# Sixty constant products in TensorE's early waits, and the turn of the outputs made on 64x128 tiles, once per group

## The chip, the core and the metric

The kernel runs on one core of a Trainium2 chip. Its engines are TensorE (PE, with the weight loads shown as PEld), VectorE (DVE), ScalarE (ACT), GpSimd (POOL) and SyncE (SP, which here only issues DMAs). Each engine works through its own queue in order, and steps on different engines are tied by semaphores. The metric is the device time of one execution in microseconds; smaller is better.

## What is computed

A gated linear attention runs over 768 tokens for 4 batches of 8 heads of width 48, and its output is the input of a feed-forward layer whose hidden value is the largest of three products.

```python
for t in range(S):
    state = alpha[:, :, t, :, None] * state + einsum('bhd,bhe->bhde', k[:, :, t], v[:, :, t])
    y[:, :, t] = einsum('bhd,bhde->bhe', q[:, :, t], state)
x = y.transpose(0, 2, 1, 3).reshape(B * S, H * D)        # 3072 x 384
h = maximum(maximum(x @ w1, x @ w2), x @ w3)             # 3072 x 768
out = h @ w_out                                          # 3072 x 384
```

## The kernel before

The work is cut into 12 groups of 256 tokens (three chunks of time by four batches, `n = 4 * c + b`). A group is two blocks of 128 tokens. The attention is done in chunks of 64 steps: decays become sums of logarithms, and q and k are scaled by their exponentials, so that a chunk is a masked product.

Each group goes through these kinds of steps. The short names are those of the code.

- `load` (SP, line 274): a, q, k, v of a group, 384 KB each; group 0 in halves of four heads.
- `aa`, `la` (351, 356, 361): the product of neighbouring decays, and logarithms. `hp` (371), `e` (378), `G` (383, 388): the totals of a chunk and their exponentials.
- `Lp` (426, a product with a constant triangle), `L0` (430), `exp` (435, ep and en), `qk` (440, on GpSimd or VectorE), `v` (259 or 261): one of two units of four heads.
- `tp` (465): turns q and k; from group 2 on both units in one step. `qkT` (479) copies that out of PSUM. `A` (491) are the scores and `LA` (499) masks them.
- `pp` (523): what the group adds to the state; `Z` (400) and `add` (412) carry the state on.
- `yi` (556) and `ya` (578): the output from the state and from the scores. `xb` (259 or 261) copies and scales a block of it; `xp` (599) turns that block with a constant matrix `order`, in three products; `xT` (255) copies the turned block.
- `gp` (622): products with the weights. The kernel uses max(x w1, x w2, x w3) = x w1 + max(0, x (w2 - w1), x (w3 - w1)): `d` (308) are the two differences, `h0` (631 or 633) and `h1` (638) the maximum, and x w1 w_out is added by `past`, a product of w1 and w_out worked out once (`wt` 322, `w1T`, `mp` 334).
- `op` (655 and 658): the last product, `ob` (255) its copy, `out` (674) the store.

`weights` (288, 291) are the four weight loads, issued on GpSimd and cast on the way: w1s (weights 0), the two halves of wcat (1 and 2), wo (3).

The order of the work isn't found by the program: the string `ORDER` lists every step with its engine and its PSUM bank (`28P0` is step 28 on TensorE, bank 0), and `Plan.emit` issues them so. There are eight banks, and a step that writes a bank waits until its last reader is done. Within an engine the order in the string is the order of its queue. Before the first `gp` TensorE has the attention of groups 0 and 1 up to the turned outputs, the first steps of group 2 and two of the three `wt`.

Of the kernel before, what the change touches and what calls it, by code (L numbers as in the profile page):

```python
# [10 lines left out]
FP32 = mybir.dt.float32  # L11
FP16 = mybir.dt.float16

AOP = mybir.AluOpType
# [9 lines left out]


ORDER = """
0S 3S 53S 6S 7S 5S 2S 1S 11V 12A 8V 13A 4S 10A 28P0 9A 54S 14P1 29V 17P2 57V 55S 30A 18V 31A 56S
59A 33V 100S 58A 60P3 75P4 19A 102S 63P5 76V 34A 101S 32V 61A 20A 103S 64V 35P6 15A 22V 145S 21V
207S 23A 36V 24P2 148S 65A 16V 40P01 146S 25V 77A 78A 147S 67G 26P6 41V 66A 275S 37P2 39G 79V 343S
42V 209S 38V 80G 208S 277S 74G 82P4 68V 69A 278S 70P2 62G 86G 210S 83V 45P0 276S 71V 81G 27V 104G  # L30
72P4 87P23 73V 46P6 50A 89V 84P4 47A 88V 85V 106A 92P7 48P0 105A 411S 49V 93P2 51P6 94V 97A 110P4
90V 98P5 111V 117P0 107P7 44V 197P2 108A 91V 52A 195P7 189V 112A 95P3 99A 118V 257P6 113A 190V 120A
261P5 258V 96A 196A 191V 325P4 122V 262A 265P3 43V 115G 119A 199P6 266A 329P7 131G 326A 121V 200A
114V 194V 124P0 116A 193V 333P5 125V 123A 330A 128V 126P3 149G 334A 132P67 127V 129P0 150A 331P5
109G 151A 198A 134V 335P3 133V 130V 162P4 137P6 267P2 163V 152P0 263P1 332V 165A 153A 192V 164A
138P5 154G 336V 259P0 211G 139A 136V 155P4 205P3 156V 213A 168G 142V 157A 203P5 161A 135V 260V 158A
166G 220P6 212A 327P7 264V 204A 143P4 268V 159G 214P0 140P1 144A 201P5 221V 141A 167V 215A 206A
227P2 393P4 160V 202A 217G 228V 169P0 279G 328V 229A 176P35 230A 173V 269P7 219G 223A 178V 347G
281A 170V 394A 177V 222A 282P2 174P0 180V 283A 225G 171P3 270A 337P6 175V 280A 232G 611S 172V 345S
288P2 181P7 224G 338A 295P0 272P1 348A 296V 231G 289V 297A 179V 349A 182P6 285V 298A 287V 234P3  # L40
291A 216V 273V 286G 340P5 183A 218G 238V 186A 274S 300G 290A 235V 344S 363P0 239P6 677S 341A 233G
364V 397P1 294A 240V 346S 226G 187P2 479S 350P3 299G 398A 399P4 545S 351A 236P5 188A 293G 400V 414S
241P71 301A 184P3 342S 401P2 242V 185A 284G 243V 413S 237V 366A 403P4 245G 402A 412S 244G 356P7
465P3 292G 480S 247V 309P25 357V 481S 466A 467P6 404V 415G 365A 548S 246V 249P3 359A 248P4 339S
310V 302P0 358A 368G 468V 546S 417A 250P 311V 416A 482S 469P7 353G 306V 313G 251A 271S 312G 461P6
303V 254A 614S 360G 470A 315V 418P2 307P3 547S 314V 462A 304P0 252P7 308V 367G 419A 255P5 463P6
253A 256A 361G 316P2 305V 317P7 362A 395P3 369G 471P4 464V 421G 352G 431P5 318P 355G 472V 354G
370P0 322A 423G 535P6 374V 319A 483G 424P4 527P7 396V 536A 549G 531P2 371V 528A 377P36 425V 430G
551A 375P0 408P7 378V 532A 379V 380G 432V 485A 381G 376V 434A 426A 533P3 436G 433A 382V 492P2 427A
372P0 383V 422G 552P5 484A 320P4 476P6 429G 493V 534V 495A 428G 321A 373V 494A 537P3 477A 435G  # L50
323P4 616A 529P2 409V 324A 538V 385P6 553A 558P0 384P1 550A 486P7 438P4 530V 487A 386P 489G 488V
437G 559V 499P3 565P7 387A 473P2 420V 390V 497G 561A 500V 439V 615G 501A 388P1 405P6 474A 566V 389A
442V 502A 491V 560A 391P2 504G 440P4 392A 593P1 441V 555G 490G 597P3 594A 445P02 568A 443P4 598A
659P1 447V 446V 617A 449G 444V 599P3 406A 496G 407S 663P0 681V 475S 661P6 664A 563V 678S 539P4 660A
498G 600V 410S 683A 564G 612S 567A 448V 618P5 679S 562G 665P0 450V 540V 680S 667P1 451V 505G 541S
666V 631P3 452P7 668A 595P4 613S 632V 619A 503V 624P2 634A 453P0 684P1 513P5 596V 621G 633A 570G
454P 685A 682A 515V 506P3 662V 458A 571G 669P1 455A 625V 635G 514V 627A 459P0 601P6 507V 626A 569G
460A 456P7 670V 542P5 602A 510V 554G 557G 628G 511P0 543A 508P2 579P6 512V 457A 630G 544S 572P4
556G 725P7 516V 509V 687G 729P0 629G 726A 603P1 730A 689G 580V 518P7 731P2 517V 581V 636G 690P3
573V 674P0 691V 582G 576V 637G 519P6 732V 583G 638P4 675A 693A 604V 520P 676S 697P0 622V 727P2 521A  # L60
524V 692A 733P1 698V 639V 699A 522P7 605P6 523A 728V 701G 734A 642V 688G 577P2 606A 574P4 585P7
578V 700A 607S 525P1 671P6 702G 526A 478S 575V 623G 584P0 703G 735P1 672A 696A 694G 673S 586P 736V
645P2 620G 643P3 686G 640P5 646V 608P1 647V 587V 641V 751P2 609A 644V 590A 740P0 610S 591P5 743P6
592V 588P1 649V 747P7 589A 648V 752V 741A 650P3 651P4 765P5 742S 695V 652P 744V 704P0 653A 711P2
656A 769P6 712V 766A 713V 657P3 705V 654P4 715G 770A 737P2 708V 658A 748A 714V 655A 706P5 709P0
717P3 707V 779P7 749P4 780A 710V 787P5 716P6 750V 763P7 718P 753P0 745P1 754V 789P4 719V 761P0 746V
783P6 722V 762A 767P1 764V 723P3 755P0 724V 738V 784V 720P7 758P3 721V 797P2 759V 771P6 788V 760S
805P7 756V 772V 785P3 757S 798V 739S 801P5 806V 781P0 768V 803P6 802V 773P2 790V 804V 799P7 782V
807P1 786V 776P5 800V 808V 791P4 774V 777V 775S 778S 813P6 792V 809P0 793S 817P3 814P 810P 815V
818P 794P7 811A 816S 812S 819V 820S 795A 796S  # L70
"""


# [41 lines left out]
def kernel(  # L115
# [12 lines left out]
    nc = tc.nc  # L128
# [14 lines left out]
    NG = NU // UB  # L143
    HG = UB * H
    TG = UB * P
    assert DM == H * D and NT == B * S


# [22 lines left out]
    ident, order, maskA = d16[:, :P], d16[:, P:2 * P], d16[:, 2 * P:]  # L171
# [9 lines left out]
    NL, NQ, NT_, HH = 5, 6, 4, H // 2  # L181
# [9 lines left out]
    xbs = homes(3, [P, P, NFT], FP16, "xb")  # L191
# [15 lines left out]
    nc.vector.memset(d16[:, :2 * P], 0.0)  # L207
    nc.vector.memset(maskA, 1.0)

    def keep(where, pattern, base, test, fill, step=-1):  # L210
# [9 lines left out]
    keep(order, [[1, P]], 0, AOP.not_equal, 1.0, -2)  # L220
    keep(order, [[1, P]], P - 1, AOP.not_equal, 1.0, -2)
    for t in las:
        nc.vector.memset(t[:, :, :, D:], 0.0)
    for t in qks:
# [55 lines left out]
    def weights(g):  # L280


        w, dst = ((moe_w1, moe_w2, moe_w3, moe_w_out)[g],
                  (w1s, wcat[:, 0], wcat[:, 1], wo16)[g])

        def run(eng):
            if g == 3:
                nc.gpsimd.dma_start(dst.rearrange("p (b s) f -> p b (s f)", s=2),
                                    w.rearrange("(b p s) f -> p b (s f)", p=P, s=2))
            else:  # L290
                nc.gpsimd.dma_start(dst.rearrange("p t f -> p (t f)"),
                                    w.rearrange("(p t) f -> p (t f)", t=NFT))
# [250 lines left out]
    def output(n):  # L543
# [42 lines left out]
                  + [("v16", u % NQ) for u in us])  # L586
        for i in range(UB):
            m = 2 * n + i
            xb, yk, xk = xbs[m % 3], keys[i], ("xp", n, i)
            plan.step("xb", "ACT DVE", rank,  # L590
                      lambda eng, xb=xb, yk=yk: scaled(
                          eng, xb.rearrange("p f t -> p (f t)"),
                          live[yk].rearrange("p a b -> p (a b)"), ysc),
                      reads=[yk], writes=[("xb", m % 3)])

            def turn(eng, xb=xb, xk=xk):
                live[xk] = bank(xk, [P, NFT, P], FP32)
                for ft in range(NFT):
                    nc.tensor.matmul(live[xk][:, ft, :], xb[:, :, ft], order,  # L599
                                     start=True, stop=True)  # L600

            plan.step("xp", "PE", rank, turn, banks=[xk], reads=[("xb", m % 3)], writes=[xk])
            to = xTs[n][:, :, i * P:(i + 1) * P]
            plan.step("xT", "DVE ACT", rank, lambda eng, to=to, xk=xk: copy(eng, to, live[xk]),
                      reads=[xk], writes=[("xT", n, i)])


    def ffn(n):
# [31 lines left out]
        for i in range(UB):  # L640
# [5 lines left out]
            for half in range(wide):  # L646
# [3 lines left out]
                for lo, hi in parts:  # L650
                    def shrink(eng, i=i, ok=ok, lo=lo, hi=hi, cols=cols):
# [5 lines left out]
                        for kt in range(lo, hi):  # L657
# [17 lines left out]
                              out[rows, cols], obs[home][:, cols]),  # L675
                          reads=[("ob", home)], size=1 / wide)

    load(0, 0, HH, "aqk")
    load(0, HH, H, "a")
    load(0, 0, HH, "v")  # L680
# [50 lines left out]
```

## Time and profile before

| | us |
|---|---|
| median of three runs | 150.99 |
| the three runs | 150.17, 150.99, 152.28 |
| span of the profiled execution | 148.5 |

The profiled execution has its span alone, from the first to the last instruction; its own device time is not listed, and the three runs lie 1.7 to 3.8 us above that span.

In the profile a row of a group reads: line, engine, operation, what it writes and reads, shapes and count; then the time busy in us, the mean of one in ns, and the idle time of the engine just before, with what ended it. In a timeline a row is the start in us, how long, the engine, the line and the count, and in brackets the idle time before it. In the chain of waits a row is a start, a length and what the end hung on there.

### The profile page before, as it was taken

What the parts mean: (1) busy time and instruction counts of PE and PEld (TensorE: products, weight loads), DVE (VectorE), ACT (ScalarE), POOL (GpSimd) and SP (SyncE); (2) the same over time, 40 slices, a digit from 0 to 9 for tenths busy, and PEclk for the clock granted to TensorE, in tenths of its full rate; (3) what the DMA queues carried; (4) which work ended last, traced back from release to release, by engine and by line L of the source; (5) the groups of instructions that cost most, each with busy time, mean ns of one, the idle gap of its engine ahead of it and who ended that gap; (6) DMA issues with size and microseconds to landing.
All of it is one profiled execution on the core that took longest, in us unless ns stands there. A gap on an engine that the chain in (4) does not pass through costs nothing.

```text
span 148.5 us, 5617 instructions
## 1 busy us (share of the span) xinstructions
PE 130.6 (88%) x2389; PEld 101.7 (68%) x2389; DVE 121.9 (82%) x231; ACT 80.7 (54%) x182; POOL 71.8 (48%) x114
## 2 busy tenths in 40 slices
PE   0136588889999999999999999999999999999990
PEld 0025576767776678887687889777777788787670
DVE  6489996999899979998896899699698786789720
ACT  3665156796895987947877759328622820000011
POOL 8105810431859888999976678994720100000000
PEclk9999999999999999999999999999999999999999
DMA  4999999999999999999997299601211100031223
GB/s 111 257 261 262 258 214 212 279 231 265 270 262 265 261 275 267 262 288 268 233 279 188 79 246 280 200 3 60 106 57 57 53 4 0 4 119 40 85 99 134
DMA packets 54728, 26.34 MB, mean 177 GB/s; under 512 B 50736, under 2 KB 54320, under 8 KB 54704
## 3 DMA queue, kind: packets, MB, share of 16 engines
q1 hardware_dynamic: 53584, 23.60, 63.4%
q0 software_dynamic: 832, 2.36, 8.1%
q8 instruction: 18, 0.29, 0.9%
q10 hardware_dynamic: 288, 0.04, 0.3%
q14 instruction: 6, 0.05, 0.1%
HBM read 23.63 MB, written 4.72 MB: 191 GB/s over the span
## 4 chain that ended last, share of the span: by engine, by line
PE 65%; DMA 10%; POOL 6%; ACT 5%; DVE 4%; SPq 4%; issue 3%; POOLq 0%; DVEq 0%
PE psum L622 26%; PE psum L658 15%; PE psum L655 8%; DMA wcat<-in_moe_w_dram 6%; SPq L274 4%; DMA qn<-in_q_dram 4%; POOL qk L440 3%; PE psum L491 3%; PE psum L578 3%; PE psum L465 2%; PE psum L599 2%; PE psum L334 2%; PE psum L556 2%; PE psum L523 2%; POOL Z L400 1%
## 5 line engine op out<-in xcount | busy, mean ns | idle before, releaser
L622 PE MATMUL psum<-xT,d 128*128 128x256 f16 x432 | 54.1, 273 | 0.9 <-DVE d L308 0.5
L622 PEld LDWEIGHTS <-d 128*128 128x128 f16 x432 | 40.0, 98 | 7.0 <-DVE d L308 1.5
L499 DVE TENSOR_TENSOR LA<-psum,d 128x1024 f16<-128x1024 f32 x24 | 28.7, 1218 | 3.7 <-PE psum L491 2.8
L658 PE MATMUL psum<-wo,hT 128*128 128x384 f16 (+1 forms) x150 | 27.5, 320 | 0.0
L638 DVE TENSOR_TENSOR hT<-psum,hT 128x512 f16<-128x512 f32 x36 | 23.7, 681 | 2.9 <-PE psum L622 2.6
L440 POOL TENSOR_TENSOR qk<-qn,ep 128x384 f16<-128x384 f32 x18 | 18.3, 1026 | 11.3 <-DMA qn<-in_q_dram 9.2
L631 ACT ACTIVATE hT<-psum 128x512 f16<-128x512 f32 x28 | 16.4, 601 | 12.7 <-PE psum L622 12.3
L255 ACT COPY ob<-psum 128x384 f32<-128x384 f32 x14 | 6.7, 481 | 27.8 <-PE psum L658 27.8
L658 PEld LDWEIGHTS <-hT 128*128 128x128 f16 x150 | 14.5, 98 | 8.9
L440 POOL TENSOR_TENSOR qk<-kn,en 128x384 f16<-128x384 f32 x16 | 15.9, 999 | 9.0 <-ACT en L435 8.5
L479 DVE COPY qkT<-psum 128x1024 f16<-128x1024 f16 x24 | 16.0, 683 | 0.9 <-PE psum L465 0.7
L655 PE MATMUL psum<-past,xT 128*128 128x384 f16 (+1 forms) x75 | 15.8, 320 | 0.0
L259 ACT ACTIVATE xb<-psum,c 128x384 f16<-128x384 f32 x17 | 9.3, 583 | 9.0 <-PE psum L578 9.0
L435 ACT ACTIVATE en<-psum 128x384 f32<-128x384 f32 x24 | 11.5, 493 | 2.1 <-DVE psum L430 2.1
L465 PE MATMUL psum<-d,qk 64*128 64x64 f16 x384 | 8.8, 198 | 4.1 <-POOL qk L440 2.1
L435 ACT ACTIVATE ep<-psum 128x384 f32<-128x384 f32 x24 | 11.6, 493 | 1.1 <-DVE psum L430 0.8
L351 POOL TENSOR_TENSOR aa<-an 128x384 f32<-128x384 f32 x9 | 9.0, 1001 | 4.7 <-DVE qkT L479 4.2
L255 ACT CAST xT<-psum 128x384 f16<-128x384 f32 x20 | 9.4, 482 | 3.0 <-PE psum L599 2.8
L426 PE MATMUL psum<-la,c 128*128 128x192 f16 x24 | 6.1, 271 | 5.5 <-ACT la L361 5.5
L465 PEld LDWEIGHTS <-qk 64*128 64x128 f16 x384 | 7.0, 99 | 5.5 <-DVE qk L440 2.9
L400 POOL TENSOR_TENSOR Z<-U,G 48x192 f16<-48x192 f32 x10 | 5.0, 504 | 11.8 <-DVE U L412 11.5
L430 DVE TENSOR_TENSOR psum<-psum,la 128x192 f32<-128x192 f32 x24 | 8.5, 358 | 2.6 <-PE psum L426 1.8
(58 smaller groups left out, 196.4 us busy)
## 6 DMA issues: line engine op xcount, KB each, us to landing
out_dram<-ob SPq DMA_DIRECT2D x23, 192.0 KB, 2.0
an<-in_alpha_dram SPq DMA_DIRECT2D x11, 384.0 KB, 6.2
qn<-in_q_dram SPq DMA_DIRECT2D x11, 384.0 KB, 5.7
kn<-in_k_dram SPq DMA_DIRECT2D x11, 384.0 KB, 6.2
vn<-in_v_dram SPq DMA_DIRECT2D x11, 384.0 KB, 6.3
wcat<-in_moe_w_dram POOLq DMA_DIRECT2D x2, 576.0 KB, 10.3
w1s<-in_moe_w_dram POOLq DMA_DIRECT2D x1, 576.0 KB, 7.9
wo<-in_moe_w_out_dram POOLq DMA_DIRECT2D x1, 576.0 KB, 7.8
```

Source lines behind the costliest of these rows:

```text
L255: (nc.scalar.copy if eng == "ACT" else nc.vector.tensor_copy)(out=out, in_=in_)
L259: nc.scalar.activation(out=out, in_=in_, func=AFT.Copy, scale=factor)
L435: lambda eng, t=t, sign=sign: nc.scalar.activation(out=t, in_=live[Lk], func=AFT.Exp, scale=sign),
L440: lambda eng, w=w, x=x, e=e: on[eng].tensor_mul(qk[:, w, :, :, :D].rearrange("p r h d -> p h r d"), ld[x][n % NL][:, hs], e),
L465: nc.tensor.transpose(live["tp", v][:, i, at:at + HALF], qks[v % NQ][rows, w, r, 2 * j:2 * j + 2, :], ident[rows, rows])
L479: lambda eng: nc.vector.tensor_copy(out=qkT.rearrange("p i w j t -> p i (w j t)"), in_=live["tp", u]),
L499: lambda eng: nc.vector.tensor_mul(LA.rearrange("p a j r t -> p (a j) (r t)"), live[Ak].rearrange("p a (j t) -> p (a j) t", j=2), maskA.un ...
L622: nc.tensor.matmul(live[gk][:, jj, :], hidden(apart[g][j][:, kt], jj), xT[:, kt, :], start=(kt == 0), stop=(kt == NFT - 1))
L631: nc.scalar.activation(out=h, in_=live[gk], func=AFT.Relu)
L638: lambda eng, h=h, gk=gk: nc.vector.tensor_max(h, live[gk], h),
L655: nc.tensor.matmul(live[ok], xT[:, kt, i * P:(i + 1) * P], past[:, kt, cols], start=(kt == 0), stop=False)
L658: nc.tensor.matmul(live[ok], hT[:, kt, i * P:(i + 1) * P], wo16[:, kt, cols], start=False, stop=(kt == NJ - 1))
```

## The change

Three things change.

1. A constant tile `filler` of ones is made, and 60 steps `dm` multiply it by itself on TensorE, 128x128 by 128x256, each into a PSUM bank that nothing reads from. All 60 are placed ahead of the first `gp`.
2. The turn of the outputs is one step `xq` per group instead of two `xp`. It works with the identity on 64 rows at a time, in 12 products, into two banks; even and odd tokens come apart in the two banks, and one `xT` copy of 128x768 puts them together. The constant `order` goes, and `xb` has four buffers for three.
3. `ORDER` is a new string: engine, bank and place are new for all steps.

```diff
-    d16 = sb.tile([P, 4 * P], FP16, name="d16")
+    d16 = sb.tile([P, 3 * P], FP16, name="d16")
+    filler = sb.tile([P, TG], FP16, name="filler")
...
+    nc.vector.memset(filler, 1.0)
...
+    def fill(i):
+        key = ("dm", i)
+        plan.step("dm", "PE", -1.0,
+                  lambda eng: nc.tensor.matmul(bank(key, [P, TG], FP32), filler[:, :P], filler,
+                                               start=True, stop=True),
+                  banks=[key], writes=[key])
...
-            def turn(eng, xb=xb, xk=xk):
-                live[xk] = bank(xk, [P, NFT, P], FP32)
-                for ft in range(NFT):
-                    nc.tensor.matmul(live[xk][:, ft, :], xb[:, :, ft], order,
-                                     start=True, stop=True)
-
-            plan.step("xp", "PE", rank, turn, banks=[xk], reads=[("xb", m % 3)], writes=[xk])
-            to = xTs[n][:, :, i * P:(i + 1) * P]
-            plan.step("xT", "DVE ACT", rank, lambda eng, to=to, xk=xk: copy(eng, to, live[xk]),
-                      reads=[xk], writes=[("xT", n, i)])
+        def turn(eng):
+            live[xk] = banks2(xk, FP32)
+            for ft in range(NFT):
+                for i in range(UB):
+                    for r in range(2):
+                        rows = slice(r * HALF, (r + 1) * HALF)
+                        at = (ft * UB + i) * HALF
+                        nc.tensor.matmul(live[xk][:, r, at:at + HALF], mine[i][rows, :, ft],
+                                         ident[rows, rows], start=True, stop=True)
+
+        plan.step("xq", "PE", rank, turn, banks=[xk],
+                  reads=[("xb", (2 * n + i) % NXB) for i in range(UB)], writes=[xk])
+        to = xTs[n].rearrange("p f (i s r) -> p r (f i) s", i=UB, r=2)
+        plan.step("xT", "DVE ACT", rank,
+                  lambda eng: copy(eng, to, live[xk][:, :, :NFT * P].rearrange(
+                      "p r (a s) -> p r a s", s=HALF)),
+                  reads=[xk], writes=[("xT", n, 0), ("xT", n, 1)], size=2.0)
```

The heads of the new orders of three queues, by kind, with the group in brackets (a half, unit or pass behind the stroke):

```
SP, new:     a(0) in two halves, a(1), a(2), q(1), q(0/0), k(0/0), k(1), q(0/1), k(0/1), v(1), v(0/1), v(0/0), q(2), k(2), a(3), v(2)
SP, old:     a(0) in two halves, a(1), k(0/1), v(0/1), q(0/1), k(0/0), q(0/0), v(0/0), q(1), k(1), v(1), a(2), k(2), q(2), v(2), a(3)
GpSimd, new: G(1), weights 0, five qk of groups 1 and 0, v(1), weights 1, weights 2, v(0), weights 3, qk(2), ...
GpSimd, old: qk(1), weights 0, qk(1), weights 1, G(1), weights 2, v(1), aa(2), qk(2), weights 3, ...
TensorE, new, up to the first gp: 7 dm, hp and Lp of groups 0 and 1, 53 dm between the steps of groups 0 and 1, three wt, xq of groups 1 and 0, tp of group 2
```

More of the change, by code (lines that the diff above doesn't have):

```diff
@@ L32 @@
[L32 to L43, printed above, removed]
@@ L71 @@
+805P0 806A 754P3 797P6 798A 724V 752V 694V 753V 755P7 695P1 696A 795V 756P 757V 799P5 800V 823P2
+824A 819P3 801P1 758A 759P5 760A 817P4 807P7 808V 815P6 833P5 825P7 816A 803P6 841P2 842A 818V 820V
+837P0 821P3 802V 843P2 839P4 835P1 822V 826V 827P7 828A 834V 830P3 796S 831A 836V 804V 809P7 775S
+829S 810A 811S 832S 812P5 813A 814S 838V 840V 845P3 844V 846P 847A 848S 853P6 854P 855A 856S 849P4
+850P 851A 852S
 """
@@ L145 @@
     TG = UB * P
+    NFILL = 60
     assert DM == H * D and NT == B * S
@@ L593, in output @@
                           live[yk].rearrange("p a b -> p (a b)"), ysc),
-                      reads=[yk], writes=[("xb", m % 3)])
-            def turn(eng, xb=xb, xk=xk):
-                live[xk] = bank(xk, [P, NFT, P], FP32)
-                for ft in range(NFT):
-                    nc.tensor.matmul(live[xk][:, ft, :], xb[:, :, ft], order,
-                                     start=True, stop=True)
-            plan.step("xp", "PE", rank, turn, banks=[xk], reads=[("xb", m % 3)], writes=[xk])
-            to = xTs[n][:, :, i * P:(i + 1) * P]
-            plan.step("xT", "DVE ACT", rank, lambda eng, to=to, xk=xk: copy(eng, to, live[xk]),
-                      reads=[xk], writes=[("xT", n, i)])
+                      reads=[yk], writes=[("xb", m % NXB)])
+        xk, mine = ("xp", n), [xbs[(2 * n + i) % NXB] for i in range(UB)]
+        def turn(eng):
[14 more added lines that the diff above has]
+                  reads=[xk], writes=[("xT", n, 0), ("xT", n, 1)], size=2.0)
     def ffn(n):
@@ L676, in ffn @@
                           reads=[("ob", home)], size=1 / wide)
+    for i in range(NFILL):
+        fill(i)
     load(0, 0, HH, "aqk")
```

85 lines of the change are left out of this document (46 added, 39 removed).

## The prediction

> **What bounds the kernel now.** I read the page's busy table first, then its slices in time, then the busy time in three stretches, then the steps around the place where the stretches change.
>
> ```profile
> span 148.5 us, 5617 instructions
> PE 130.6 (88%) x2389; PEld 101.7 (68%) x2389; DVE 121.9 (82%) x231; ACT 80.7 (54%) x182; POOL 71.8 (48%) x114
> PE   0136588889999999999999999999999999999990
> PEclk9999999999999999999999999999999999999999
> DMA  4999999999999999999997299601211100031223
> ...
> 26.00:30.00 4.00, 3.52 (x34) 1.00 1.18 275
> 30.00:40.00 10.00, 9.15 (x190) 1.00 1.10 255
> 40.00:146.00 106.00, 104.90 (x1863) 1.00 0.61 157
> sum 26.00, PE 13.00; mean PE 2.60
> ...
> 26.04 0.83 PE L622 MATMUL psum<-xT,d 128*128 128x256 f16 x6 [0.51 <-DVE d L308]
> 144.20 0.99 PE psum L658 x6
> ```
>
> The kernel has two parts. Up to 26.04 us, when the first expert product (line 622) starts, TensorE is half idle: 13.00 us busy of 26. From there to the last product, which ends at 145.2 (144.20 + 0.99), it works almost without a gap: 3.52 + 9.15 + 104.90 = 117.6 us busy of 119.2, 1.6 idle. After it come 3.3 us of copy, store and end. So the span is a start (26.0), TensorE's work (117.6), its gaps (1.6) and a tail (3.3), together 148.5. A change can move the first three. The shown runs are 1.7 to 3.8 us above the span, their median 2.5; I add 2.5.
>
> What makes the start 26 us long?
>
> ```profile
> 10.00:15.00 5.00, 2.75 (x94) 2.14 (x88) 4.73 (x10) 2.14 (x5) 2.23 (x3) 1.00 1.27 263
> 15.00:20.00 5.00, 3.21 (x113) 2.78 (x117) 4.90 (x6) 0.95 (x2) 3.68 (x6) 1.00 1.19 244
> ...
> 12.73 1.38 POOL L440 TENSOR_TENSOR qk<-qn,ep 128x384 f16<-128x384 f32 x1 [8.45 <-DMA qn<-in_q_dram]
> 14.05 0.74 POOL L291 DMA_DIRECT2D w1s<-in_moe_w_dram  x1
> 15.62 0.61 ACT L259 ACTIVATE v<-vn,c 128x384 f16<-128x384 f32 x1 [2.37 <-DMA vn<-in_v_dram]
> 15.77 9.15 DMA wcat<-in_moe_w_dram
> 25.42 0.56 DVE L308 TENSOR_TENSOR d<-wcat,w1s 128x768 f16<-128x768 f16 x1 [1.18 <-DMA wcat<-in_moe_w_dram]
> q0 software_dynamic: 832, 2.36, 8.1%
> w1s<-in_moe_w_dram POOLq DMA_DIRECT2D x1, 576.0 KB, 7.9
> 17.78 11.01 SPq L274 DMA_DIRECT2D an<-in_alpha_dram  x2
> ```
>
> Columns after the stretch are the five engines PE, PEld, DVE, ACT, POOL. Two things run level: VectorE, busy 4.73 and 4.90 of each 5 us, and the DMA engines. Loads land at a steady pace: group 1's q, the end of the sixth full load in SP's order, by 12.6, and its v, the end of the eighth, by 15.6, so 1.5 us for a load. The four weight transfers take 8.1% of the engines' span, 12.0 us, 3.0 each, and they push the loads aside: SP needs 11 us from 17.78 for two issues. The last wait before the first product is VectorE's 1.18 us for wcat. TensorE is not on this chain.
>
> **The sixty products.** Seven stand ahead of all TensorE work and 53 more between there and the first expert product; none stands after it. They have 128x256 operands, as line 622 has.
>
> ```profile
> 40.36 0.65 PE psum L622 x6
> L321 PE MATMUL psum<-d,w1s x18: 219/314/314, 23.8 to 29.6; 128*128 128x128 f16 x18
> ```
>
> At 0.65/6 = 0.11 us each they are 6.5 us. The row of line 321 shows that early products are slower: 314 ns in the median and first, 219 at the fastest, while the page's granted clock reads 9 in every slice; the slices do not tell this apart. So a fill can cost up to twice 0.11, 13 us in all, about the 13.0 us that TensorE idles before 26.04. I cost them at nothing, since the idle time hides them. Without that cover they cost at most those 13 us less the idle part; the rival below prices it. [...]
>
> Each fill writes a bank of PSUM and so waits for that bank's last reader. One stands ahead of group 2's hp and two w1 turns, waiting for a masking on VectorE (line 499); hp and what is behind it use the same banks and would wait anyway. I add nothing.
>
> **The new start.** Prices from the groups by shape:
>
> ```profile
> L430 DVE TENSOR_TENSOR psum<-psum,la 128x192 f32<-128x192 f32 x24 | 8.5, 358 | 2.6 <-PE psum L426 1.8 <-ACT la L356 0.7
> L479 DVE COPY qkT<-psum 128x1024 f16<-128x1024 f16 x24 | 16.0, 683 | 0.9 <-PE psum L465 0.7
> L499 DVE TENSOR_TENSOR LA<-psum,d 128x1024 f16<-128x1024 f32 x24 | 28.7, 1218 | 3.7 <-PE psum L491 2.8 <-issue 0.7
> L440 DVE TENSOR_TENSOR qk<-kn,en 128x384 f16<-128x384 f32 x8 | 5.2, 659 | 0.0
> L440 DVE TENSOR_TENSOR qk<-qn,ep 128x384 f16<-128x384 f32 x6 | 3.2, 553 | 0.4 <-DMA qn<-in_q_dram 0.2
> L400 DVE TENSOR_TENSOR Z<-psum,G 48x192 f16<-48x192 f32 x8 | 2.8, 355 | 0.3
> L412 DVE TENSOR_TENSOR V<-psum,Z 48x192 f32<-48x192 f32 x16 | 5.5, 351 | 0.3
> L261 DVE TENSOR_SCALAR xb<-psum,c 128x384 f16<-128x384 f32 x7 | 4.3, 611 | 0.2
> L255 DVE CAST xT<-psum 128x384 f16<-128x384 f32 x4 | 2.2, 555 | 0.8 <-PE psum L599 0.8
> L255 ACT COPY w1T<-psum 128x768 f16<-128x768 f16 x3 | 2.4, 815 | 0.0
> ```
>
> VectorE first. In the new order its steps between group 0's first k half and the first d are 3 L0, 4 qkT, 4 LA, 4 qk (three q, one k), 1 w1T, 4 Z, 3 add, 2 xb. That is 3 x 0.358 + 4 x 0.683 + 4 x 1.218 + 3 x 0.553 + 0.659 + 0.6 + 4 x 0.355 + 3 x 0.351 + 2 x 0.611 = 15.3 us. (A w1T copy on VectorE is not in the trace: between 0.555, half the size from 32-bit, and 0.815 on ScalarE; I take 0.6, near the first.) That k half now ends the fifth full load's worth: two halves of alpha and one full make two, alpha of group 2 three, q of group 1 four, two halves five. So it lands one load before 12.6, at 11.1; its qk takes 0.66, and the sum ends at 27.1. In the same stretch VectorE idled 0.37 us in 10, so some 0.5 more, less about as much for the overlap of neighbours: first d at 27.1, with 26.5 and 28.5 as ends.
>
> Now the weights. GpSimd issues w1s (weights 0) right after G of group 1, before its first qk, so at about 9 us instead of 14.05. The other two are moved behind five qk and a v step on GpSimd's queue; the last of these waits for group 1's v, the eighth load as before: 15.6 plus the 3.0 us that weights 0 takes out of the loads, 18.6. With 0.6 for v the issue comes at 19.2 instead of 15.77. A weight transfer lands 7.9 us after its issue: 27.1, and VectorE starts d some 0.45 after such a landing (24.92 to 25.42), 27.5. So both lines meet; the first product follows d by 0.6 (25.42 to 26.04): **28.1 us, 2.1 later than now** (ends +0.9 and +3.5). SP's order moves alpha of group 2 and q of group 1 ahead of halves of group 0; group 1's v ends the same volume, so nothing else follows there. xT of group 0 is no later: xb ends near 25.7 in VectorE's list, then 0.2 for the turn and at most 2 x 0.48 for the copy.
>
> **TensorE's work after the first product.** Counted in the two orders from there on: 20 old turns become 10 new ones of 12 small products, one w1 turn of six products and one merged tp step of 32 go ahead of it; all else is equal.
>
> ```profile
> 43.17 0.57 PE psum L465 x32
> 45.76 0.75 PE psum L491 x32
> 48.41 0.49 PE psum L655 x3
> 50.38 0.47 PE psum L465 x32
> 50.85 0.59 PE psum L655 x3
> 53.61 0.17 PE psum L599 x3
> L255 ACT CAST xT<-psum 128x384 f16<-128x384 f32 x20 | 9.4, 482 | 3.0 <-PE psum L599 2.8
> ```
>
> An old turn is 0.17, so 20 are 3.4 us. A new product has the shape of line 465's, 64 rows by 128, 64 moving: 0.47/32 = 15 ns, 10 x 12 are 1.8 (at most 23 ns, the slowest small ones of line 491, 2.8). Gain 1.6. The w1 turn is worth 0.34 (two of 0.17), the tp 0.47.
>
> Against it stands a row: three products of line 655 take 0.49 after full-size work and 0.59 after line 465, and line 465 itself 0.47 after small work and 0.57 after line 622. So each change between full and small tile shapes costs 0.10. The old turn was full-size as its neighbours; the new one is not. Changes of shape in TensorE's order after the first product: 55 before, 64 after, 9 x 0.10 = +0.9. [...] Sum: -1.6 - 0.34 - 0.47 + 0.9 = **-1.5 us** (ends -2.4, without the changes of shape, and -0.5).
>
> The copies of xT fall from 24 to 12, all on ScalarE, each between 0.815 and 0.96 in place of two of 0.48; with VectorE's list shorter by three ob, two xb, four xT and a relu, and longer by one aa, w1T and past, VectorE loses over 4 us of work. That is off TensorE's path; it helps the 1.6 us of gaps. I take them at 0.6, **-1.0** (ends -1.6 and +0.5).
>
> **Sum:** 148.5 + 2.1 - 1.5 - 1.0 = 148.1; with 2.5 around it, 150.6: no change that can be measured. About 2% (3 us) is what a measurement can tell: three runs of the same kernel lie 1.4% apart.
>
> **Rivals.**
> *The start is not later, and the gaps close (faster).* If VectorE's list overlaps more than I allow and the w1 transfer comes with less than 7.9 us because no other weight is ahead of it, the first product stays at 26.0; the gaps go to nothing and the shape changes cost half: 148.5 - 1.9 - 1.6 = 145.0, as a run 147.5. For it: the wait at 25.42 was short, and VectorE has less to do. Against it: the later issue. Chance 0.22.
> *Group 2's k is starved (slower).* The k load stands three full loads behind group 1's v in SP's order: 18.6 + 4.5 = 23.1. The three weight transfers follow each other from about 19.2 on and take 9 us. If the first of them begins over an us before 23.1 minus its own start-up, k lands only after all three, near 31. VectorE's qk for it stands ahead of the first d, and tp of group 2 ahead of the first product, so that would start near 32.5: +6.5 - 1.5 - 1.0 = 152.5, as a run 155.0. For it: SP's 11 us for two issues. Against: weights 0 issued at 14.05 landed at 22, so 3 us of transfer started near 19, five us after the issue; the same lag puts this one at 24. Chance 0.10.
> *The fills stand in the way.* If TensorE stays slow, 13 us of fills beside 13 of work fill the start, and each step of the early chain waits behind a few: up to 2 us more: 150.1, as a run 152.6. Chance 0.13.
> *The turns gain nothing.* With products at 23 ns the work falls by 0.5 only: 149.1, as a run 151.6. Chance 0.10.
>
> **How the numbers follow.** The forecast has 0.45; it and the two last rivals lie within 2%, the first rival just past it on the fast side, half the cost of each end of the start (0.9 to 3.5) inside. Faster 0.22, same 0.67, slower 0.11. The range leaves out the starved case and the outer part of the fast one: 147.2 to 153.0.
>
> **What would show it.** In the new profile the first product of the expert group should start at 27 to 29, after a wait of VectorE for wcat of under an us or none; w1s should land well before; the fills should lie in TensorE's idle time; a turn of twelve should take 0.2 to 0.3; TensorE should be idle for under an us after the first product. A first product at 26 or before, or beyond 30, makes the sum wrong; so does TensorE work after it that is not 1 to 2 us less.

## The result and the profile after

| | before | after |
|---|---|---|
| median, us | 150.58 (150.07 to 152.28, 4 runs) | 158.97 (158.34 to 160.55, 4 runs) |
| ratio to before | 1 | 1.0538, 95% interval 1.045 to 1.0627 |
| span of the profiled execution, us | 148.5 | 157.4 (that execution as a run: 159.07) |

The change makes the kernel 5% slower; 150.6 was forecast, with 153.0 as the upper end. The page of the kernel after, its first lines and the slices of TensorE and its clock:

```profile
span 157.4 us, 5883 instructions
PE 140.3 (89%) x2521; PEld 105.0 (67%) x2521; DVE 124.0 (79%) x225; ACT 88.1 (56%) x182; POOL 69.7 (44%) x107
PE   4099896799978899998899999799999999999992
PEclk9999999869999999999999999999999999999999
```

TensorE's row has digits of 7 and 8 well into the second quarter and again in the middle, where the row of before had nines, and the clock shows an 8 and a 6 in the two slices from 27.5 to 35.4 us. Busy time by stretch of the kernel after (first column the stretch, then its length, PE, PEld, DVE, ACT, POOL, granted clock, DMA share, GB/s):

```profile
26.00:30.60 4.60, 2.04 (x63) 1.45 (x63) 2.60 (x7) 1.98 (x3) 0.00 (x0) 1.00 1.09 205
30.60:34.00 3.40, 3.04 (x16) 1.95 (x15) 3.37 (x8) 1.68 (x3) 0.66 (x1) 0.50 1.15 277
...
31.74:154.40 122.66, 118.30 (x2105) 90.41 (x2104) 101.15 (x172) 72.37 (x149) 56.25 (x81) 0.99 0.60 152
...
40.00:55.00 15.00, 12.86 (x268) 9.13 (x267) 14.71 (x27) 11.80 (x29) 8.94 (x12) 1.00 0.94 220
...
95.00:100.00 5.00, 3.87 (x58) 2.71 (x56) 4.49 (x6) 2.25 (x6) 4.85 (x10) 1.00 0.85 220
```

The first expert product (now line 642) starts at 31.74 in place of 26.04: 5.7 of the 8.9 us. From it to the end of TensorE's work the stretch is 122.66 in place of 119.16. TensorE is busy for 118.30 of it, 0.7 more than before, and idle for 4.36 in place of 1.6. The tail is 3.0 for 3.3. Together: 5.7 + 0.7 + 2.8 - 0.3 = 8.9.

The stretch from 40 to 55 shows who is late there: VectorE is busy for 14.71 of 15 us while TensorE loses 2.1. In the start, TensorE idles for over half of the 4.6 us before 30.6, then works 3.4 us at half the clock. The timeline there (start, length, engine, line, count; in brackets the idle time before):

```profile
25.43 0.55 PE L589 MATMUL psum<-v,LA 64*128 64x48 f16 x30
28.37 0.20 PE L589 MATMUL psum<-v,LA 64*128 64x48 f16 x2 [2.38 <-issue]
...
29.10 0.79 ACT L258 COPY w1T<-psum 128x768 f16<-128x768 f16 x1
...
29.78 1.91 ACT L258 CAST xT<-psum 128x768 f16<-128x768 f32 x2
...
30.37 1.03 DVE L319 TENSOR_TENSOR d<-wcat,w1s 128x768 f16<-128x768 f16 x2
...
31.74 4.52 PE L642 MATMUL psum<-xT,d 128*128 128x256 f16 x30 [0.36 <-ACT xT L258]
```

In the middle of one step (ya of group 0, 32 products) TensorE stands still for 2.38 us, and the trace names no releaser ("issue"). All that follows is late by it: xb, the turn, then on ScalarE a w1T copy and two xT copies in a row, and the first product waits for the last of these. VectorE's groups that changed most (line, operation, shapes, count; then busy us and mean ns):

```profile
L394 DVE TENSOR_TENSOR G<-e 128x4 f32<-128x4 f32 x5 | 3.7, 739 | 0.0
L399 DVE TENSOR_TENSOR H<-e,e 128x4 f32<-128x4 f32 x2 | 2.3, 1130 | 0.0
L411 DVE TENSOR_TENSOR Z<-V,H 48x192 f16<-48x192 f32 x2 | 1.9, 940 | 0.0
```

G and H have four columns and took 272 and 146 ns before; a Z from V took 350. They now take up to 1.67 us (G), 1.28 (H) and 1.22 (Z).

### The profile page after: what moved, and what is told of

Its sections match the earlier page's. It is cut to its first block, busy times and chain, and to the rows that moved or that the text cites. A ratio compares the mean times of both kernels' runs of the same rounds, so it can differ in the third digit from the quotient of the medians.

```text
span 157.4 us, 5883 instructions
## 1 busy us (share of the span) xinstructions
PE 140.3 (89%) x2521; PEld 105.0 (67%) x2521; DVE 124.0 (79%) x225; ACT 88.1 (56%) x182; POOL 69.7 (44%) x107
## 4 chain that ended last, share of the span: by engine, by line
PE 63%; DVE 17%; ACT 6%; issue 6%; DMA 3%; SPq 2%; DVEq 0%; ACTq 0%
PE psum L642 25%; PE psum L678 11%; PE psum L675 6%; DVE LA L510 4%; PE psum L303 3%; DMA qn<-in_q_dram 3%; PE psum L476 3%; PE psum L502 3%; PE psum L589 3%; SPq L277 2%; DVE hT L658 2%; ACT xT L258 2%; DVE qk L451 2%; PE psum L534 2%; PE psum L567 2%
## 5 line engine op out<-in xcount | busy, mean ns | idle before, releaser
L642 PEld LDWEIGHTS <-d 128*128 128x128 f16 x432 | 41.5, 99 | 9.4 <-issue 2.8
L651 ACT ACTIVATE hT<-psum 128x512 f16<-128x512 f32 x29 | 17.0, 600 | 21.1 <-PE psum L642 16.6
L451 POOL TENSOR_TENSOR qk<-kn,en 128x384 f16<-128x384 f32 x20 | 20.1, 1015 | 17.4 <-ACT en L446 9.3
L678 PE MATMUL psum<-wo,hT 128*128 128x384 f16 (+1 forms) x150 | 27.5, 320 | 0.0
L451 POOL TENSOR_TENSOR qk<-qn,ep 128x384 f16<-128x384 f32 x15 | 14.9, 999 | 6.5 <-ACT ep L446 3.6
L303 PE MATMUL psum<-filler 128*128 128x256 f16 x60 | 13.7, 354 | 2.1 <-DVE filler L211 1.3
L262 ACT ACTIVATE xb<-psum,c 128x384 f16<-128x384 f32 x19 | 10.3, 581 | 8.8 <-PE psum L589 8.8
L258 ACT CAST xT<-psum 128x768 f16<-128x768 f32 x12 | 12.2, 1027 | 5.0 <-PE psum L616 4.4
L258 ACT COPY ob<-psum 128x384 f32<-128x384 f32 (+1 forms) x17 | 7.7, 462 | 12.7 <-PE psum L678 11.8
L362 POOL TENSOR_TENSOR aa<-an 128x384 f32<-128x384 f32 x8 | 9.7, 1213 | 8.8 <-DMA an<-in_alpha_dram 8.8
L502 PE MATMUL psum<-qkT 48*64 48x128 f16 x384 | 8.9, 223 | 0.7 <-DVE qkT L490 0.6
```

The lines of the kernel that those rows point to most:

```text
L258: (nc.scalar.copy if eng == "ACT" else nc.vector.tensor_copy)(out=out, in_=in_)
L303: lambda eng: nc.tensor.matmul(bank(key, [P, TG], FP32), filler[:, :P], filler, start=True, stop=True),
L451: lambda eng, w=w, x=x, e=e: on[eng].tensor_mul(qk[:, w, :, :, :D].rearrange("p r h d -> p h r d"), ld[x][n % NL][:, hs], e),
L642: nc.tensor.matmul(live[gk][:, jj, :], hidden(apart[g][j][:, kt], jj), xT[:, kt, :], start=(kt == 0), stop=(kt == NFT - 1))
L651: nc.scalar.activation(out=h, in_=live[gk], func=AFT.Relu)
L678: nc.tensor.matmul(live[ok], hT[:, kt, i * P:(i + 1) * P], wo16[:, kt, cols], start=False, stop=(kt == NJ - 1))
```

## The experiments

The runs are told by cause: first the small VectorE steps, then the constant products; the turn and its copies come in between, in e9, e10 and e7. Ratios are to the kernel before, on the same chip. Spans, windows and timelines are those of one profiled execution of each run. In the diffs of `ORDER` only the entries that change are shown; they stand apart in the string.

### Small VectorE steps beside GpSimd

**e4.** Eight steps that the new order gives to VectorE (six G or H, two Z) go to GpSimd, in the same places of the order.

```diff
-269V 208V 401V 466V 469V 596V 726V 724V
+269G 208G 401G 466G 469G 596G 726G 724G
```

> The changed kernel with six small products of factors (G) and two state steps (Z) moved from VectorE back to GpSimd at the same places of the order. Theory C (contention): these steps took 0.7 to 1.4 us on VectorE where they met a GpSimd step, against 0.15 to 0.35 alone, and VectorE is what TensorE waits for at 41 to 54, 70 to 76 and 95 to 100 us; the span falls by 2 to 3 us, to 154.5 to 155.5. Rival: VectorE is late for other reasons, span 156.5 to 158.

153.18 us, ratio 1.0139 (0.9954 to 1.0324), span 152.0. Windows of this run:

```profile
31.45:149.00 117.55, 117.17 (x2105) 90.08 (x2104) 94.18 (x164) 71.85 (x149) 58.73 (x89) 0.99 0.63 159
```

Six steps at 0.15 and two at 0.35 are 1.6 us of work, but VectorE's busy time falls by 7.0, from 101.15 to 94.18, and TensorE's idle time from 4.36 to 0.4. The stop in the start stays (2.3 us). So these eight steps cost 5.4 us of span (5.8 by the medians, with two executions of e4), twice what was expected.

**e8.** The other way round in the old order: seven of the G and H steps that GpSimd has there go to VectorE.

```diff
-109G 217G 353G 352G 555G 554G 620G
+109V 217V 353V 352V 555V 554V 620V
```

> The kernel before with its own order, but seven of the fourteen small totals of a chunk (128x4, two inputs in SBUF) that GpSimd makes after the first expert product moved to VectorE, in the same places of the order. If such a step on VectorE waits until the running GpSimd step has ended, their mean goes from 0.15 us to 0.5-1.0, and the span grows by 1 to 4 us, ratio 1.01 to 1.03. If the small steps cost only their own work, 7 x 0.15 = 1 us is added on VectorE, which is idle for 18 of the 119 us, and the span grows by less than 0.5, ratio under 1.005.

150.54 us, ratio 0.9981 (0.9941 to 1.0022): the expected cost is not there. The rows of this run say why:

```profile
L383 DVE TENSOR_TENSOR G<-e 128x4 f32<-128x4 f32 x8 | 2.2, 272 | 0.0
L388 DVE TENSOR_TENSOR H<-e,e 128x4 f32<-128x4 f32 x4 | 0.6, 154 | 0.0
```

In the old order GpSimd is idle, or inside a step of at most 0.7 us, when they run; the one that met a qk (107.64) met its last 0.2 us. The engine alone is not the cause; what GpSimd does at that moment is. In the kernel after they look like this, VectorE's row and GpSimd's row in pairs:

```profile
47.81 0.98 DVE L399 TENSOR_TENSOR H<-e,e 128x4 f32<-128x4 f32 x1
47.77 1.00 POOL L451 TENSOR_TENSOR qk<-qn,ep 128x384 f16<-128x384 f32 x1 [1.56 <-ACT ep L446]
...
51.05 1.37 DVE L394 TENSOR_TENSOR G<-e 128x4 f32<-128x4 f32 x1
51.40 0.99 POOL L362 TENSOR_TENSOR aa<-an 128x384 f32<-128x384 f32 x1
```

H begins 0.04 after GpSimd's qk and ends at 48.79, 0.02 after that ends (48.77). G begins inside another qk and ends at 52.42, 0.03 after the aa that follows it (52.39): it waited through two GpSimd steps.

**e14.** Is it the reading of two tensors from SBUF that makes the step wait? In the kernel after, each G or H on VectorE becomes four products of one column, with the second factor as a scalar per partition: one tensor read from SBUF, not two.

```diff
-on[eng].tensor_mul(G, x, y)
+for j in range(NP):
+    nc.vector.tensor_scalar(out=G[:, j:j + 1], in0=x[:, j:j + 1], scalar1=y[:, j:j + 1],
+                            scalar2=1.0, op0=AOP.mult, op1=AOP.mult)
```

> The changed kernel with one thing changed: where a small total of a chunk (128x4) is made on VectorE, it is made by four products of one column each, with the second factor as a scalar per partition, so that each instruction reads one tensor from SBUF and a scalar, not two tensors. If these steps are slow because their two inputs need something that the running GpSimd step holds, none of the four is stretched: each takes 0.06 to 0.2 us, six steps cost 1.5 to 4 us on VectorE in place of 5.8, and the span falls by 1.5 to 4 from 157.4. If they are slow for another reason (they wait for ScalarE's e, or any VectorE step beside GpSimd is slow), the four together take at least as long, and the span stays at 157 or rises.

156.5 us, ratio 1.031 (1.0201 to 1.042), span 155.0. The same two places in this run:

```profile
47.50 0.57 DVE L410 TENSOR_SCALAR H<-e,e 128x1 f32<-128x1 f32 x4
47.46 1.00 POOL L462 TENSOR_TENSOR qk<-qn,ep 128x384 f16<-128x384 f32 x1 [1.56 <-ACT ep L457]
...
50.33 0.57 DVE L410 TENSOR_SCALAR G<-e 128x1 f32<-128x1 f32 x4
50.00 0.99 POOL L462 TENSOR_TENSOR qk<-kn,en 128x384 f16<-128x384 f32 x1
```

Four instructions of one input take 0.56 or 0.57 together at each of seven places, five of them beside a GpSimd step, and none is stretched. A Z from V and H, left as it was, took 1.9 us there. TensorE's idle time after its first expert product is 2.4 (4.36 before the edit). The kernel after itself has a second sign: VectorE's two-input steps that take one input from PSUM are not stretched either, in any of 24 executions each (nanoseconds, shortest, median and longest):

```profile
L441 DVE TENSOR_TENSOR psum<-psum,la x24: 348/356/367, 8.1 to 113.7; 128x192 f32<-128x192 f32 x24
L510 DVE TENSOR_TENSOR LA<-psum,d x24: 1202/1215/1226, 13.8 to 128.8; 128x1024 f16<-128x1024 f32 x24
```

The one at 74.92, for example, took 0.35 us although a qk and then an aa ran on GpSimd. So the small step was stretched where it read two tensors from SBUF while GpSimd worked: 0.15 us alone (the G at 22.87 and 131.26 of the kernel after), 0.35 to 1.67 beside GpSimd; with one tensor and a scalar it was not. What in the chip makes it wait is not shown.

### The constant products, the turn and its copies

**e1.** No constant products, else the new order.

```diff
-    NFILL = 60
+    NFILL = 0
```

> The changed kernel without the sixty constant products; every other step, its engine, bank and order stay. Theory S (supply): the fills use up TensorE's instruction buffer early; its third refill came only at 26.1 us, behind the weight transfers, so TensorE stood 2.4 us and its clock fell to half from 30.6 to 34.0. Then without fills the stop near 26 us is gone, the first expert product starts at 28.5 to 29.5 instead of 31.7, and the span is 152 to 154. Theory O (order): the new order itself is late, and the fills only sit in idle time. Then the first product stays after 31 and the span is 156 to 158.

157.18 us, ratio 1.0404 (1.023 to 1.0578), span 155.2, first expert product at 29.32. The products cost 2.2 us of span (1.8 by the medians, with two executions of e1). The stop without a releaser is still there, but is 0.82 us.

**e5.** The kernel before, with sixty such products put into its own order ahead of the first expert product, three to eleven at a place.

> The kernel before with the same sixty constant products put into its own order ahead of the first expert product, each in the bank of the next step. Theory S: TensorE's instructions run out 120 earlier, while the three weight transfers hold the DMA engines from 17 to 28 us; a stop of 1 to 4 us shows up ahead of or among the first expert products, span 149.5 to 152. Theory O: the fills sit in idle time, the clock is at full speed earlier, span 147 to 149.

150.37 us, ratio 0.9974 (0.9931 to 1.0017). In the old order they cost nothing, and TensorE has no such stop.

**e6.** e4 and e1 together: eight steps on GpSimd, no constant products.

> The changed kernel with both earlier edits at once: the eight small two-input steps on GpSimd instead of VectorE, and no constant products. If the two costs are separate, their gains add: the span falls by 5.4 and by 2.2 from 157.4, to about 149.8, with the first expert product at 29.3 and TensorE idle for under 1 us after it; ratio to before about 1.00. If the fills cost time only because VectorE was late anyway (one cost seen twice), the span stays at 152, as with the eight steps alone, ratio about 1.014.

152.53 us, ratio 1.0148 (1.0074 to 1.0221), span 150.5, first product at 29.23. The start gains its 2.2 (from 31.45), but TensorE's stretch after it is 0.7 longer than in e4: the span gains 1.5 of the 2.2, and the medians 0.65 (153.18 to 152.53). The next run shows where the rest went.

**e9.** e6 with the turn as six full 128x128 products per group with the constant `order`, and the copy of xT contiguous.

```diff
-nc.tensor.matmul(live[xk][:, r, at:at + HALF], mine[i][rows, :, ft], ident[rows, rows], ...)
+nc.tensor.matmul(live[xk][:, i, ft * P:(ft + 1) * P], mine[i][:, :, ft], order, ...)
```

> The kernel with eight steps on GpSimd and without constant products, and with the turn made as six full 128x128 products per group with the constant order, as before the change, and the copy of xT contiguous; steps, engines and order stay. If the small tiles gain what was forecast, full ones cost TensorE about 10 x (0.34 - 0.27) = 0.7 us more, less up to 9 changes of tile shape at 0.10: within 0.5 us of the run without this edit. The copies of xT on ScalarE should fall from 0.95-1.04 to about 0.82. If the strided copy sits in the chain of waits at the start (two copies ahead of the first product), the first product comes 0.3 earlier.

150.59 us, ratio 1.0019 (0.9974 to 1.0063), span 149.2, a larger gain than expected. First e6, then e9, the first expert products in the timeline and the window of all work from there on, and the group of the xT copies in e9:

```profile
29.23 5.07 PE L639 MATMUL psum<-xT,d 128*128 128x256 f16 x30
...
29.23:147.50 118.27, 117.85 (x2105) 90.37 (x2104) 94.54 (x164) 71.88 (x149) 57.46 (x89) 1.00 0.63 163
```

```profile
29.03 3.44 PE L638 MATMUL psum<-xT,d 128*128 128x256 f16 x30 [0.39 <-ACT xT L257]
...
29.03:146.20 117.17, 116.83 (x2045) 91.18 (x2044) 94.78 (x165) 70.06 (x149) 57.69 (x89) 1.00 0.66 167
```

```profile
L257 ACT CAST xT<-psum 128x768 f16<-128x768 f32 x12 | 9.5, 804 | 5.4 <-PE psum L612 5.4
```

In e6 the first expert products take 169 ns each (5.07 / 30), in e9 115 (3.44 / 30). TensorE was still slow in e6, where small turns, with two waits of 0.5 us beside them, precede them; in e9 1.7 us of full products do. The page's clock has nines there in both, but nines are also what it shows where the trace has no entry for the clock. The first entry, of full speed, begins at 32.60 us in e6 and at 28.31 in e9 (25.54 in the kernel before, 16.93 in the kernel after). Split at 32.60, the products of e6 take 198 ns each up to there (3.37 / 17) and 100 in the 1.4 us after it (1.40 / 14); in e4, where the entry is 0.50 until 33.52, they take 207 (2.07 / 10). So e6 makes its expert products at the slow clock for 3.4 us, a loss of some 1.7, and e4 for 2.1, a loss of some 1.0: the missing 0.7. Whether the small shape of the turns or the waits beside them kept the clock down in e6 is not shown. The contiguous copy takes 804 ns for the 1027 of the strided one.

**e10.** e9 with the last w1T copy moved ahead of the four xb copies on ScalarE, into an idle stretch (`188A` ahead of `92A`).

> The kernel with eight steps on GpSimd, no constant products and full-size turns (span 149.2, first expert product at 29.03), with one step moved: the copy of the last w1T goes ahead of the four xb copies on ScalarE, into an idle stretch of 2.05 us there. If the start hangs on ScalarE's row w1T, xT(1), xT(0), the row begins 0.8 earlier for xT(1), xT(0) then follows its turn at once, and the first product comes at 28.2 with the span at 148.4, ratio to before 0.995. If the weights or VectorE's d (ready at 29.15 for the first two, but only the first is needed) set it, the first product stays within 0.3 of 29.0.

150.18 us, ratio 0.9979 (0.9947 to 1.001), span 148.6, first product at 28.40: 0.6 of the 0.8 expected; it now waits 0.29 us for VectorE's d. This is the fastest form of the new order, and level with the kernel before. **e7**, the same aim by copying xT of group 0 first and w1T last, went wrong:

> The kernel of the run above (eight steps on GpSimd, no constant products) with one thing changed: ScalarE copies xT of group 0 first, then xT of group 1, then the last w1T, where the order of the change has w1T, xT(1), xT(0). If the start hangs on the two 0.95 us copies and the w1T copy that stand ahead of xT(0) on ScalarE, the first expert product comes at 28.3 instead of 29.3 and the span falls by about 1.0. If it hangs on the weights or on tp of group 2, both unchanged, nothing moves by more than 0.3.

153.83 us, ratio 1.0231 (1.0163 to 1.0298). tp of group 2, ahead of the first product, writes the bank that w1T is copied from, and TensorE waited 2.64 us for w1T. The expectation took tp of group 2 as unchanged, and it was not.

**e11.** e10 with the sixty products back.

> The kernel of the run above with the sixty constant products put back in the places that the change gave them. If TensorE's instruction buffer runs dry because sixty products and sixty weight loads are added ahead of the stretch in which the weights land, TensorE again stands still for over 2 us near 26 with no releaser, the first product comes 1.5 to 2.5 later than without them, and the clock falls to half for 3.4 us afterwards: span 2 to 3.5 above the run without. If the stop in the changed kernel came only from its late start, the sixty products cost under 0.5, and the full clock that they bring earlier (products of line 321's kind at 219 instead of 310 ns) may gain up to 1.

152.93 us, ratio 1.0156 (1.0116 to 1.0195). TensorE stops for 2.03 us at 24.79, again after the 30th product of ya, and has half the clock from 26.4 to 29.8. The row of the stop, with the idle time in brackets:

```profile
26.82 0.22 PE L592 MATMUL psum<-v,LA 64*128 64x48 f16 x2 [2.03 <-issue]
```

So the products cost time also where nothing else is late: 2.75 us by the medians (152.93 against 150.18), 1.4 by the two profiled spans (150.0 against 148.6).

**e12.** e11 with every second product only, each 512 columns wide. Its profiled execution was the longest of twelve (154.51 us), so only the times are compared.

> The kernel of the run above with every second constant product only, each twice as wide (512 columns): the same array time, half the instructions. If the number of instructions is what runs TensorE dry, the stop of over 2 us is gone and the first product comes within 0.8 of the kernel without fills; if it is the array's time that the fills take, the time stays that of the sixty narrow ones.

151.11 us, ratio 1.0037 (1.0 to 1.0073): with the same time in the array (the constant products are busy for 12.7 us in both) and half the instructions, 0.9 us instead of 2.75. The number of instructions matters. **e2**, the same thirty wide products in the kernel after as it was, had a stop of 0.59 us instead of 2.38, and the time of e1, which has no constant products: there the wide ones cost nothing that can be told.

> Thirty constant products of 512 columns in place of sixty of 256: the same time on TensorE, half the instructions (60 fewer). Theory S: the stop moves by some 60 instructions, past the turns, to about 28 to 31 us, or is shorter; the first product is earlier than 31.7 by 1 to 2.5 us; span 154 to 156.5. Rival F (the fills' time stands in the way, not their count): nothing changes, first product at 31 to 32, span 157 to 158. Theory O: as rival F.

157.13 us, ratio 1.0401 (1.0234 to 1.0567).

**e13.** e11 with weights 1, 2 and 3 issued behind qk of group 2 on GpSimd.

```diff
-127G 132G 144G 94G 187G 178G
+127G 94G 178G 132G 144G 187G
```

> The kernel with all sixty constant products, full-size turns, eight steps on GpSimd and the early w1T copy (TensorE stops for 2.03 us at 24.79 with no releaser, first product at 30.39), with one thing changed: GpSimd issues weights 1, 2 and 3 after qk of group 2 instead of before v(0), so that they start some 2 us later. If TensorE stops because the next 16 KB of its instructions stand behind the weight transfers on the DMA engines, these 16 KB now pass before the weights, the stop is under 0.5 us, and the start is set by the weights instead (first product between 29.5 and 31.5). If TensorE stops for another reason, after a fixed number of instructions or as a pause of the engine itself, the stop of 2 us is still there.

155.95 us, ratio 1.0324 (1.0249 to 1.0399): the weights are now late, and the first product starts at 33.26. The stop shrinks to 0.79, neither under 0.5 nor 2. The windows from 0 to just before TensorE goes on, in the kernel after, in e6 and in e13:

```profile
0.00:28.30 28.30, 19.17 (x351) 12.73 (x352) 19.75 (x47) 12.30 (x28) 13.48 (x26) 1.00 1.07 229
```

```profile
0.00:28.80 28.80, 14.37 (x351) 10.98 (x352) 21.94 (x53) 15.01 (x32) 13.45 (x26) 1.00 1.04 228
```

```profile
0.00:26.90 26.90, 19.07 (x351) 12.64 (x352) 19.71 (x47) 13.00 (x29) 14.10 (x29) 1.00 1.02 233
```

The counts in brackets are the point: TensorE stops after 351 products and 352 weight loads in each of them, with the constant products and without (e6 has none of the sixty among its 351); the stop is at a fixed count of its instructions. And the DMA queues of the kernel after, first from 18.9 to 26.05, then from 26.05 to 28.3, then of e13 from 19.1 to 24.4 and from 24.4 to 26.9 (packets, MB, share of the 16 engines):

```profile
q0 software_dynamic: 239, 1.03, 72.7%
q1 hardware_dynamic: 1686, 0.63, 41.8%
...
q0 software_dynamic: 181, 0.35, 82.7%
q1 hardware_dynamic: 182, 0.07, 17.4%
q8 instruction: 1, 0.02, 2.6%
```

```profile
q1 hardware_dynamic: 3264, 1.23, 100.5%
...
q1 hardware_dynamic: 1590, 0.60, 94.1%
q8 instruction: 1, 0.02, 2.5%
```

A packet of instructions passes shortly before TensorE goes on, after a long stretch in which the engines are full of other transfers and no such packet passes. By the packet times in the traces it ends at 27.03 in the kernel after, and TensorE goes on at 28.37. Nine kernels stop at this count (the kernel after, e1, e2, e4, e6 and e11 to e14), and in all of them TensorE goes on 1.3 to 1.7 us after the end of that packet. Where the packet is early enough there is no stop: in e5 it ends at 23.48, and TensorE comes to the place at 24.85. So it is this piece of instructions that TensorE waits for; the sixty products, with sixty loads, bring it to the end of what it has before the next piece is there.

What sets the time of that piece is not settled. In e13 the transfers beside it are loads, and it begins at 24.45, as in e11; the stop is shorter because TensorE comes to that place 1.35 later (26.14 against 24.79). That does not clear the weights: with TensorE behind by 1.35, the piece came no later. That full DMA engines delay it is argued, not shown.

## Why the prediction was wrong

**The start, +2.1 forecast, +5.7 measured.** The two lines it was built on held within their ends: the first d, forecast at 27.5 from the weights and 27.1 from VectorE's list, came at 27.90 in e1, where no stop of TensorE precedes it. e1, timeline:

```profile
27.19 1.90 ACT L255 CAST xT<-psum 128x768 f16<-128x768 f32 x2
...
27.90 1.03 DVE L316 TENSOR_TENSOR d<-wcat,w1s 128x768 f16<-128x768 f16 x2
...
29.07 0.32 PE L473 MATMUL psum<-d,qk 64*128 64x64 f16 x5 [0.82 <-issue]
```

The step that failed is the one that left the rest of the chain out: "xT of group 0 is no later", with a copy of at most 2 x 0.48, and "TensorE is not on this chain". In the kernel after, xT of group 0 is the last thing there, behind a w1T copy (0.79) and the other xT, at 1.03 each for the strided form. By the forecast's terms xT of group 0 was due at 26.9 (25.7 + 0.2 + 0.96); in e1 it was ready at 29.09, and the last xb before it at 26.74; TensorE, back from its stop at 29.07, then had five products of another step left before the first expert product. And TensorE is on the chain now: in the kernel after, the last xb waits 1.93 us for the products behind the stop. Without the constant products the first product comes at 29.2 or 29.3 (e6, e1); with the contiguous copy and an earlier w1T at 28.4. That this is 0.3 from the 28.1 of the forecast takes two edits which the forecast did not have.

**The fills "at nothing" was the second failed step: 0.65 to 2.75 us by the medians of three pairs of kernels, 1.4 to 2.2 by their spans.** They fit the idle time of TensorE's array, as said (the sixty are busy for 13.7 us in the kernel after, for "13 us in all"), and the rival "the fills stand in the way" (+2.0) had about the right size, but for another reason: not steps queued behind slow products, but instructions that have not arrived. They did make the products of the start faster: the w1 turns took 219 ns each in the kernel after and 310 in e1, in the mean (the rows have shortest, median and longest; first the kernel after, then e1).

```profile
L332 PE MATMUL psum<-d,w1s x18: 216/219/219, 20.4 to 22.2; 128*128 128x128 f16 x18
...
L329 PE MATMUL psum<-d,w1s x18: 268/314/314, 19.3 to 21.8; 128*128 128x128 f16 x18
```

Then that was lost again: half the clock for 3.41 us, from 30.58 to 34.00, just when the expert products begin, 151 ns each (4.52 / 30) for the 115 of e9. What makes the clock fall is not shown. In the kernel after it fell 2.2 us after the end of a stop of 2.38 us, in e11 within a stop of 2.03; in e2 it halves at 28.49, with TensorE busy for 1.96 of the 3.41 us before and no stop over 0.67.

**TensorE's work, -1.5 forecast, +0.7 measured.** The turns take 0.17 to 0.31 us in e4's chain of waits, five of nine 0.29, where 0.18 + 0.10 was the sum. In e4, whose eight steps are out of the way, TensorE is busy for 117.17 against 117.57, and some 1.0 of it is the half clock: 1.4 less at full clock, so -1.5 holds there. The kernel after is busy for 1.1 more than e4, and the clock accounts for 0.1 of that; the rest went with the eight steps, and how it came about is not shown. Full-size turns (e9) give 116.83 at full clock, so the small tiles bring some 0.7 of it, which is the 1.6 less 0.9 of the forecast. The strided copy and the slower clock behind them, which the forecast did not have, took more than that.

**The gaps, -1.0 forecast, +2.8 measured.** This is the largest failure, 5.4 us of span by e4. The prediction counted what VectorE loses ("over 4 us of work") with the prices of before. The count holds: with the eight steps (1.6 at the prices of before) on GpSimd, VectorE's work after the first product is 7.0 lower than before, 94.18 for 101.23 (5.4 lower with those 1.6 added), and TensorE's idle time is 0.4, below the 0.6 of the forecast. The prices don't hold: steps of 0.15 and 0.35 us took up to 1.67 because the order puts them beside GpSimd's long steps. The forecast looked for a new wait only in the start; the rival on the slow side was not it: qk of group 2's k ran on GpSimd from 23.5 on, and the rival had 31 for the landing.

**By sum:** eight steps 5.4, fills 1.5, the small turn with its strided copy and the clock behind it 1.3, w1T's place 0.6, from 157.4 down to 148.6 in e4, e6, e9 and e10, against 148.5 before. These are spans of one execution each; the medians of the same runs give 5.8, 0.65, 1.9 and 0.4, so only the first term is much larger than what lies between executions of one kernel, and the small ones are rough. What the new order gains after its first product (117.18 us in e10 for 119.16) is about what its later start takes (+2.4). No version beat the kernel before by more than can be told.

## What to carry to other kernels

Before pricing a step by its row, look at what the other engine does at that moment: here a VectorE step of 0.15 us with two inputs in SBUF took up to 1.67, and ended 0.02 or 0.03 after GpSimd's step (H at 47.81, G at 51.05); with such steps on GpSimd the span fell by 5.4 us (e4), and with one input they took 0.57 at most (e14). Work that fills an engine's idle time is not free because the array is idle: it takes instructions, and they must have arrived; sixty products cost 2.75 us in e11, thirty of twice the width 0.9 in e12. And for each step called "no later", write down the whole row of copies ahead of it on its engine, and the buffer that each one frees.

## What was not expected of the hardware

- TensorE stopped at the same count, 351 products and 352 loads, in nine of the kernels that were run, for 0.5 to 3.4 us (3.42 in e14), and went on 1.3 to 1.7 us after a 16 KB piece of instructions had passed. The profile shows it only as "issue".
- The granted clock halved for 3.41 us in the kernel after, from 30.58 (its stop of 2.38 us ended at 28.37), for 3.4 in e11, from 26.4 (its stop of 2.03 ended at 26.82), and in e2 from 28.49, with no stop over 0.67 before.
- In the kernel after, a VectorE step waited through two GpSimd steps in a row: the longest G, at 97.08, took 1.67 us and ended 0.03 after the second of two qk of 0.99 us each.
- A ScalarE copy of 128x768 from PSUM took 804 ns with neighbouring elements written side by side (e9), and 1027 with every second one (the kernel after).
